# Converting the gated stage's weights beside the experts instead of beside the attention

## The chip, the core and the metric

The kernel runs on one core of one Trainium2 chip, as one launch. The core has a matrix engine (TensorE, PE in the rows), a vector engine (VectorE, DVE), an activation engine (ScalarE, ACT), a general engine (GpSimd, POOL) and a queue engine (SyncE, SP) that issues most DMA transfers. Each of them works through its own queue in program order. The metric is device time in microseconds (us) of the whole launch; every number below is from the kernel before unless it says otherwise.

## What is computed

Three stages follow one another: an attention with pooled queries, a layer of eight experts of which each token takes one, and a gated layer.

```python
# attention: batch 4, heads 8, sequence 1152, head size 64
q_pool = q.reshape(B, H, S // 2, 2, D).mean(axis=3)
scores = np.matmul(q_pool, k.transpose(0, 1, 3, 2)) / np.sqrt(D)
scores = scores - np.max(scores, axis=-1, keepdims=True)
attn = np.exp(scores)
attn = attn / (np.sum(attn, axis=-1, keepdims=True) + 1e-09)
x = np.matmul(attn, v)                  # -> 2304 tokens of 512
# experts: w_gate 512 x 8, w1[e] 512 x 1024, w2[e] 1024 x 512
expert_idx = np.argmax(x @ w_gate, axis=1)
for e in range(8):
    mask = expert_idx == e
    out[mask] = gate_w[mask, None] * (np.maximum(x[mask] @ w1[e], 0.0) @ w2[e])
# gated layer: w_a, w_b 512 x 1536, w_out 1536 x 512
y = ((out @ w_a) * (out @ w_b)) @ w_out
```

The weights w_a, w_b and w_out of the gated layer arrive as float64. [...]

## The kernel before

**Attention.** The 32 heads are handled in 16 pairs of heads (NPAIR), each pair in 21 units (NU), so that 336 units run one after the other. For unit n, TensorE computes scores (`scores`, L335 and L338, PSUM tile sp, two buffers), ScalarE takes the exponential twice, as float32 (L345, tile pt) and as its float16 high half (L347, tile ph), GpSimd subtracts the two to get the low half (`p_low`, L365, tile pl), and four units later TensorE multiplies both halves with the values (`av`, L387). The row maxima of the next pair are found beside that (`a_units`): TensorE computes rough scores (L289) into the PSUM tile sa, which has two buffers, and VectorE reduces each of them to maxima (L294, tile mx). Around this, VectorE also splits keys, values and queries into high and low halves (L228, L214, L242), normalises the results of the pair before (`norm`, `norm_tail`, L407 to L424), and every fourth pair computes the gate (`gate`).

**Conversion.** The three weights are cut into 36 parts of 128 x 512 numbers (`parts`: 12 blocks f, each with m = 0, 1, 2 for w_a, w_b, w_out). For each part SyncE loads the 64-bit words into the tile cl (`conv_load`, L640), ScalarE takes the absolute value of the upper words (`conv_abs`, L649, tile mag), and VectorE runs five instructions: it limits mag (L656), takes the sign from the upper words (L657, tile sgn), adds bits of the lower words (L662), shifts mag (L669) and puts the two together (L674). SyncE then writes the float32 part to a DRAM tile wf (L675). `conv` is a generator with four steps; the call `aside()` in the loop over the units takes one step of the gate, and where no gate is open, one step of the conversion. The list ASIDE holds 0, 1 or 2 for each of the 21 units, 12 steps in all for a pair, from unit 10 on.

**Experts.** The tokens are sorted by expert into slots of 128 (`do_slot`; 18 always run, up to 25 where needed). A slot gathers its tokens (L958, GpSimd's queue), turns them (`x_t`, L971), multiplies by w1 (`stage1`), takes the relu (L991, tile hs), turns the result (`h_t`, L997), multiplies by w2 (`stage2`), scales and scatters (`finish`, L1013, L1014). Each product runs on high and low halves, three matmuls (L977 to L979). The halves come from a cast on ScalarE (hh, xh: L964) and a subtraction on VectorE (hl, xl: L965). Where the next slot has another expert (`changes`), the 16 pieces of its weights are split in the same way (`split_w`: L716 on ScalarE, L720 on VectorE, a quarter of the latter on GpSimd), and the weights after next are loaded (`load_raw`, L141, 1 MB each on SyncE). The first 12 parts of the gated weights (RES = 4 blocks) are read back from wf in slots 0 to 11 (L622, tile pre) and split at the end of the slot (`part_split`, L631 on ScalarE, L632 on VectorE, tile wch, wcl).

**Gated layer.** It runs six blocks of 384 tokens over the 12 blocks f (`ab`, `outs`). The other 24 parts are read back from wf and split while the first block of tokens runs.

The code is issued in the order in which it is written (a manual schedule); no planner reorders it.

## Time and profile before

| what | us |
|---|---|
| median of three runs | 1427.13 (1422.78 to 1430.41) |
| the profiled execution | 1423.17, span 1421.1 |
| attention, from the start to its last pair (from 594.8) | 594.8 |
| last pair, routing, up to the experts' first transposition | 594.8 to 647.7 |
| experts | 647.7 to 948.2 |
| gated layer | 948.2 to 1421.1 |

The profile is one execution with a record for each instruction. TensorE is busy for 90% of the span, VectorE for 59%, ScalarE for 46%, GpSimd for 39%. By 40 equal slices VectorE is at nine tenths through most of the attention and at one to three tenths in the last third. Busy shares of TensorE are to be read with care: its matmuls are pipelined, and their ends are modelled.

### The profile page before, as it was taken

What the parts mean: (1) busy time and instruction counts of PE and PEld (TensorE: products, weight loads), DVE (VectorE), ACT (ScalarE), POOL (GpSimd) and SP (SyncE); (2) the same over time, 40 slices, a digit from 0 to 9 for tenths busy, and PEclk for the clock granted to TensorE, in tenths of its full rate; (3) what the DMA queues carried; (4) which work ended last, traced back from release to release, by engine and by line L of the source; (5) the groups of instructions that cost most, each with busy time, mean ns of one, the idle gap of its engine ahead of it and who ended that gap; (6) DMA issues with size and microseconds to landing.
All of it is one profiled execution on the core that took longest, in us unless ns stands there. A gap on an engine that the chain in (4) does not pass through costs nothing. (4 is left out here: it accounts for less than half of the span.)

```text
span 1421.1 us, 28742 instructions
## 1 busy us (share of the span) xinstructions
PE 1275.9 (90%) x10800; PEld 1018.5 (72%) x10800; DVE 834.0 (59%) x1388; ACT 656.8 (46%) x1295; POOL 556.6 (39%) x467
## 2 busy tenths in 40 slices
PE   8688888878878988858998999989999999999998
PEld 6455555555555555536876887779999999999998
DVE  5689999999998989886279226325322222222211
ACT  3467776766767766834267226224212112111211
POOL 4567787777777777873145113210000000000000
PEclk9999999998999999978999999999999999999999
DMA  6768786567566765134359314424010101010000
GB/s 158 156 158 198 189 223 157 153 161 180 129 153 146 194 141 117 46 136 154 115 178 346 133 47 158 165 70 150 21 45 1 45 1 45 1 45 1 23 0 23
DMA packets 184497, 162.16 MB, mean 114 GB/s; under 512 B 102864, under 2 KB 138192, under 8 KB 184336
## 3 DMA queue, kind: packets, MB, share of 16 engines
q1 hardware_dynamic: 180496, 147.14, 38.1%
q0 software_dynamic: 3840, 13.00, 2.7%
q8 instruction: 86, 1.41, 0.4%
q14 instruction: 75, 0.61, 0.1%
HBM read 106.07 MB, written 25.48 MB: 93 GB/s over the span
## 5 line engine op out<-in xcount | busy, mean ns | idle before, releaser
L365 POOL TENSOR_TENSOR pl<-pt,ph 128x512 f16<-128x512 f32 (+1 forms) x333 | 414.3, 1260 | 167.0 <-ACT ph L347 128.0
L345 ACT ACTIVATE pt<-sp 128x512 f32<-128x512 f32 (+1 forms) x336 | 197.8, 589 | 161.5 <-PE sp L338 150.2
L289 PE MATMUL sa<-kst,qq 128*128 128x384 f16 x480 | 164.2, 342 | 82.8 <-DVE mx L294 78.8
L1144 PE MATMUL ab<-x,wch 128*128 128x384 f32 x1152 | 236.5, 336 | 0.7 <-ACT x L1127 0.7
L294 DVE TENSOR_REDUCE mx<-sa 128x2 f32<-128x768 f32 x224 | 205.4, 922 | 37.3 <-PE sa L289 34.8
L387 PEld LDWEIGHTS <-ph 128*128 128x128 f16 (+1 forms) x2880 | 157.8, 103 | 77.9 <-issue 38.7
L1144 PEld LDWEIGHTS ab<-x,wch 128*128 128x128 f32 x1152 | 202.6, 188 | 5.9 <-ACT x L1127 1.1
L1154 DVE TENSOR_TENSOR gf<-ab,sa 128x384 f32<-128x384 f32 x72 | 40.1, 557 | 272.3 <-PE ab L1144 272.3
L347 ACT ACTIVATE ph<-sp 128x512 f16<-128x512 f32 (+1 forms) x315 | 186.0, 590 | 0.0
L387 PE MATMUL av<-vv,ph 128*128 128x65 f16 (+2 forms) x2880 | 174.9, 199 | 0.0
L289 PE MATMUL sa<-kst,qlt 128*128 128x384 f16 x480 | 164.5, 343 | 0.0
L387 PE MATMUL av<-vv,pl 128*128 128x65 f16 (+1 forms) x1440 | 161.7, 197 | 2.4 <-DVE pl L365 1.7
L335 PE MATMUL sp<-qq,kst 128*128 128x512 f16 (+1 forms) x576 | 141.1, 299 | 10.8 <-ACT ph L347 10.3
L338 PE MATMUL sp<-rl,k2b 66*128 66x512 f16 (+1 forms) x576 | 141.2, 299 | 6.4 <-DMA rl<-qln 6.4
L387 PEld LDWEIGHTS <-pl 128*128 128x128 f16 (+1 forms) x1440 | 126.9, 104 | 2.8 <-DVE pl L365 1.8
L289 PEld LDWEIGHTS <-qlt 128*128 128x128 f16 x480 | 48.3, 101 | 109.4 <-issue 90.4
L1144 PE MATMUL ab<-x,wcl 128*128 128x384 f32 x576 | 123.6, 335 | 0.0
L1153 ACT COPY sa<-ab 128x384 f32<-128x384 f32 x72 | 34.6, 481 | 163.8 <-PE ab L1144 163.8
L1155 ACT CAST gh<-gf 128x384 fp32r<-128x384 f32 x72 | 37.0, 513 | 149.3 <-DVE gf L1154 149.3
L1144 PEld LDWEIGHTS ab<-x,wcl 128*128 128x128 f32 x576 | 103.2, 188 | 0.0
L965 DVE TENSOR_TENSOR hl<-ht,hh 128x512 fp32r<-128x512 f32 x46 | 31.6, 688 | 107.6 <-ACT hh L964 107.6
L1014 POOL DMA_INDIRECT ybuf<-ys,idx x23 | 25.5, 1111 | 165.1 <-DVE ys L1013 122.3
(187 smaller groups left out, 2412.7 us busy)
## 6 DMA issues: line engine op xcount, KB each, us to landing
raw<-in_moe_w_dram SPq DMA_DIRECT2D x36, 1024.0 KB, 6.8
kr<-in_k_dram SPq DMA_DIRECT2D x16, 576.0 KB, 5.2
vr<-in_v_dram SPq DMA_DIRECT2D x16, 576.0 KB, 5.8
wf<-mag SPq DMA_DIRECT2D x36, 256.0 KB, 3.0
qr<-in_q_dram SPq DMA_DIRECT2D x32, 256.0 KB, 3.5
cl<-in_moe_w_a_dram SPq DMA_DIRECT2D x12, 512.0 KB, 4.7
cl<-in_moe_w_b_dram SPq DMA_DIRECT2D x12, 512.0 KB, 3.9
cl<-in_moe_w_out_dram SPq DMA_DIRECT2D x12, 512.0 KB, 3.8
```

The costliest lines, as they stand in the source:

```text
L289: nc.tensor.matmul(sa[:, i, :KA], lhsT=x[:, 128 * b_ : 128 * b_ + 128], rhs=kst[:, j, ks], start=o == 0, stop=o == len(ops) - 1,)
L294: nc.vector.tensor_reduce(out=s["mx"].rearrange("p t n -> p (t n)")[:, ones[0] : ones[0] + m].rearrange("p (m o) -> p m o", o=1), in_=sa[: ...
L335: nc.tensor.matmul(sp[:, o : o + w], lhsT=s["kst"][:, j, ks], rhs=s["qq"][:, c0 : c0 + w], start=True, stop=False)
L338: nc.tensor.matmul(sp[:, o : o + w], lhsT=k2b[p % 3][:, j, ks], rhs=s["rl", j if w > 64 else 1][0:66, c0 : c0 + w], start=False, stop=True,)
L345: nc.scalar.activation(pt[:, :o], sp[:, :o], AF.Exp, scale=1.0 / (16.0 * SC * SC))
L347: nc.scalar.activation(phb[n % NPB][0][:, :o], sp[:, :o], AF.Exp, scale=1.0 / (16.0 * SC * SC))
L365: eng.tensor_tensor(out=l[:, :w], in0=pts.pop(n)[:, :w], in1=h[:, :w], op=ALU.subtract)
L387: nc.tensor.matmul(o, lhsT=a, rhs=b_, start=first, stop=False, skip_group_check=True)
L1144: nc.tensor.matmul(ps[:, 0:TB], lhsT=w_[:, m, 128 * i : 128 * i + 128], rhs=x_[:, i], start=(i + j == 0), stop=(j == 2 and i == KD - 1),)
L1153: nc.scalar.copy(sa, pair[0])
L1154: nc.vector.tensor_tensor(out=gf, in0=pair[1], in1=sa, op=ALU.mult)
L1155: nc.scalar.copy(gh, gf)
```

## The change

The conversion leaves the attention and goes to the experts. `aside` now takes steps of the gate alone. In `do_slot`, a new function `beside(s, 3)` stands at three places (after the first `h_t`, after the second, and behind `finish`) and takes three conversion steps at each for slots 0 to 16, twelve for slot 17. The tiles mag, sgn and cl move to the experts' pools mp and mp2, with two buffers of mag in place of three. Part 0 gets two steps of its own for the first loads and the first Abs. The first 12 parts are no longer written to wf and read back: a fifth step splits them straight from mag with `part_split`. The other 24 still go through wf. The tile pre is gone for this kind of weights.

```diff
--- before.py
+++ after.py
@@ -636,23 +636,31 @@
 
     def conv_load(i):
         f, m = parts[i]
-        t = pst[i] = er2.tile([128, 512], I64, tag="cl", name=f"cl{i}")
+        t = pst[i] = cvp["2"].tile([128, 512], I64, tag="cl", name=f"cl{i}")
         nc.sync.dma_start(out=t.rearrange("p (k f) -> p k f", k=KD) if m < 2 else t, in_=chunk_src(f, m))
 
 
     mags = {}
+    cvp = {}
 
     def conv_abs(i):
         if i < len(parts):
-            mags[i] = er.tile([128, 512], F32, tag=f"mag{i % 3}", name=f"mag{i}")
+            mags[i] = cvp["1"].tile([128, 512], F32, tag=f"mag{i % 2}", name=f"mag{i}")
             bits = pst[i].bitcast(U32).rearrange("p (n w) -> p n w", w=2)
             nc.scalar.activation(mags[i], bits[:, :, 1].bitcast(F32), AF.Abs)
 
+
     def conv(i):
         f, m = parts[i]
+        if i == 0:
+            conv_load(0)
+            conv_load(1)
+            yield
+            conv_abs(0)
+            yield
         bits = pst.pop(i).bitcast(U32).rearrange("p (n w) -> p n w", w=2)
         mag = mags.pop(i)
-        sgn = er.tile([128, 512], U32, tag="sgn", name=f"sgn{i}")
+        sgn = cvp["1"].tile([128, 512], U32, tag="sgn", name=f"sgn{i}")
         nc.vector.tensor_scalar(out=mag, in0=mag, scalar1=W_LO, scalar2=W_HI, op0=ALU.max, op1=ALU.min)
         nc.vector.tensor_scalar(
             out=sgn, in0=bits[:, :, 1], scalar1=0x80000000, scalar2=0x40000000,
@@ -672,19 +680,23 @@
         )
         yield
         nc.vector.tensor_tensor(out=mag.bitcast(U32), in0=mag.bitcast(U32), in1=sgn, op=ALU.bitwise_xor)
-        nc.sync.dma_start(out=wf[f, m], in_=mag)
+        if i < 3 * RES:
+            yield
+            part_split(i, wres, mag)
+        else:
+            nc.sync.dma_start(out=wf[f, m], in_=mag)
         yield
 
 
     gates = []
+
     convs = [conv(i) for i in range(len(parts))] if wide else []
 
-    def aside():
-        for todo in (gates, convs):
-            while todo:
-                if next(todo[0], todo) is None:
-                    return
-                todo.pop(0)
+    def aside(todo=gates):
+        while todo:
+            if next(todo[0], todo) is None:
+                return
+            todo.pop(0)
 
     a_first = [3 * t + n for t in (0, 1, 2, 3) for n in range(3)]
     a_rest = [3 * t + n for t in (4, 5, 6, 7, 8) for n in range(3)]
@@ -818,11 +830,6 @@
                     finish_max(pa, (0, 1) if pa else [1])
             if a_due(n + 1) < a_due(n) + 2 and n + 1 < NPAIR * NU:
                 scores(n + 1)
-            if n == 6 and wide:
-                for i in range(2):
-                    conv_load(i)
-            if n == 9 and wide:
-                conv_abs(0)
             if u == (U["lv"] if p else 5) and nxt:
                 load_v(p + 1)
             for j in range(2):
@@ -894,7 +901,7 @@
                 aside()
             if p == NPAIR - 1:
                 if u == 0:
-                    while gates or convs:
+                    while gates:
                         aside()
                     w1h, w1l, w2h, w2l = open_mw()
                 for i in range(L_H[u], L_H[u + 1]):
@@ -938,6 +945,8 @@
     mp2 = mo_ctx.enter_context(tc.tile_pool(name="mp2", bufs=2))
     mp3 = mo_ctx.enter_context(tc.tile_pool(name="mp3", bufs=4))
     mps = mo_ctx.enter_context(tc.tile_pool(name="mps", bufs=1, space=PSUM))
+    cvp["1"] = mp
+    cvp["2"] = mp2
 
     def split_w(i, ks=(0, 1, 2, 3)):
         for k_ in ks:
@@ -1042,10 +1051,15 @@
                 load_raw(i, next_e(0))
         x_t(0)
         pre = {}
+
+        def beside(s, n):
+            for _ in range(n if s < NT // 128 - 1 else 4 * n if s < NT // 128 else 0):
+                aside(convs)
+
         def do_slot(s):
             if s + 2 < NS:
                 gather(s + 2)
-            if s < 3 * RES:
+            if s < 3 * RES and not wide:
                 pre[s] = mp2.tile([128, 512], F32, tag="pre", name=f"pre{s}")
                 part_src(pre[s], s)
             if s:
@@ -1058,6 +1072,7 @@
                     split_w(3, [0])
             stage1(s, 1, [0, 1])
             h_t(s, 0)
+            beside(s, 3)
             stage1(s, 1, [2, 3])
             if s:
                 with tc.If(changes(s) > 0):
@@ -1065,6 +1080,7 @@
                     load_raw(3, next_e(s))
             stage2(s, [0, 1])
             h_t(s, 1)
+            beside(s, 3)
             if s + 1 < NS:
                 x_t(s + 1)
                 with tc.If(changes(s + 1) > 0):
@@ -1073,8 +1089,9 @@
                         load_raw(i, next_e(s + 1))
             stage2(s, [2, 3, 4, 5, 6, 7])
             finish(s)
-            if s < 3 * RES:
+            if s < 3 * RES and not wide:
                 part_split(s, wres, pre.pop(s))
+            beside(s, 3)
 
         def live(s):
             return nc.values_load(info[0:1, 2, s : s + 1], engines=wengs + [ET.PE], min_val=0, max_val=1)
```

In the rows that follow, names are tiles, with numbers that tell copies apart.

VectorE's queue in the attention, during pair 6, before: mx are the maxima of pair 7, vv and kn the split values and keys, mag, sgn and cl the conversion.

```order
L294 TENSOR_REDUCE mx_4168<-sa_4_4274 128x2
L662 SCALAR_TENSOR_TENSOR sgn_4258<-cl_3878,sgn_4258 128x512
L669 TENSOR_SCALAR mag_4152<-mag_4152 128x512
L674 TENSOR_TENSOR mag_4152<-mag_4152,sgn_4258 128x512
L294 TENSOR_REDUCE mx_4168<-sa_6_4328 128x2
L228 SCALAR_TENSOR_TENSOR kn_4311<-kr_4009,kn_4311 128x9x64
L294 TENSOR_REDUCE mx_4168<-sa_8_4362 128x2
L656 TENSOR_SCALAR mag_4289<-mag_4289 128x512
L657 TENSOR_SCALAR sgn_4376<-cl_4150 128x512
L228 SCALAR_TENSOR_TENSOR kn_4311<-kr_4009,kn_4311 128x9x64
L294 TENSOR_REDUCE mx_4168<-sa_10_4424 128x2
```

The same place after:

```order
L294 TENSOR_REDUCE mx_4010<-sa_4_4111 128x2
L294 TENSOR_REDUCE mx_4010<-sa_6_4157 128x2
L228 SCALAR_TENSOR_TENSOR kn_4142<-kr_3860,kn_4142 128x9x64
L294 TENSOR_REDUCE mx_4010<-sa_8_4191 128x2
L228 SCALAR_TENSOR_TENSOR kn_4142<-kr_3860,kn_4142 128x9x64
L294 TENSOR_REDUCE mx_4010<-sa_10_4250 128x2
```

Five conversion instructions between the reductions are gone; the rest stands in the same order.

VectorE's queue in slot 7 of the experts, from the first half's low part (hl) to the next slot's tokens (xl), before. The rows with a load, a compare and branches are the test whether the expert changes:

```order
L965 TENSOR_TENSOR hl_0_12624<-ht_0_12618,hh_0_12623 128x512
L1029 TENSOR_LOAD info
L1063 COMPARE_AND_BRANCH
L720 TENSOR_TENSOR w2l<-raw_133,w2h 128x512 x2
L1063 UNCONDITIONAL_BRANCH x2
L965 TENSOR_TENSOR hl_1_12679<-ht_1_12673,hh_1_12678 128x512
L965 TENSOR_TENSOR xl_12688<-xt_12682,xh_12687 128x512
```

The same slot after, from the middle of the first three conversion steps to xl:

```order
L682 TENSOR_TENSOR mag_12183<-mag_12183,sgn_12271 128x512
L1038 TENSOR_LOAD info
L1078 COMPARE_AND_BRANCH
L732 TENSOR_TENSOR w2l<-raw_133,w2h 128x512 x2
L1078 UNCONDITIONAL_BRANCH x2
L974 TENSOR_TENSOR hl_1_12416<-ht_1_12410,hh_1_12415 128x512
L664 TENSOR_SCALAR mag_12359<-mag_12359 128x512
L665 TENSOR_SCALAR sgn_12419<-cl_12181 128x512
L670 SCALAR_TENSOR_TENSOR sgn_12419<-cl_12181,sgn_12419 128x512
L677 TENSOR_SCALAR mag_12359<-mag_12359 128x512
L974 TENSOR_TENSOR xl_12434<-xt_12428,xh_12433 128x512
```

Conversion instructions now stand in front of the weight split (w2l), of hl and of xl.

ScalarE's queue in slot 6, from the first half's cast (hh) to the next slot's tokens (xh), before:

```order
L964 CAST hh_0_12398<-ht_0_12393 128x512
L991 ACTIVATE hs_1_12408<-hp_1_12386 128x512
L1029 TENSOR_LOAD info
L1063 COMPARE_AND_BRANCH
L716 CAST w2h<-raw_133 128x512 x3
L1063 UNCONDITIONAL_BRANCH x2
L964 CAST hh_1_12453<-ht_1_12448 128x512
L964 CAST xh_12462<-xt_12457 128x512
```

The same slot after; wch is the high half of a part, cast from mag:

```order
L973 CAST hh_0_12110<-ht_0_12105 128x512
L650 ACTIVATE mag_12116<-cl_11936 128x512
L631 CAST wch_12024<-mag_11938 128x512
L1000 ACTIVATE hs_1_12128<-hp_1_12098 128x512
L1038 TENSOR_LOAD info
L1078 COMPARE_AND_BRANCH
L728 CAST w2h<-raw_133 128x512 x3
L1078 UNCONDITIONAL_BRANCH x2
L973 CAST hh_1_12173<-ht_1_12168 128x512
L650 ACTIVATE mag_12183<-cl_12114 128x512
L973 CAST xh_12191<-xt_12186 128x512
```

An Abs and the cast of a part now stand in front of the relu (hs), and a second Abs in front of xh.

## Rows read from the trace of the kernel before

**Rows 1.** The page: span, and busy time of each engine.
```profile
span 1421.1 us, 28742 instructions
PE 1275.9 (90%) x10800; PEld 1018.5 (72%) x10800; DVE 834.0 (59%) x1388; ACT 656.8 (46%) x1295; POOL 556.6 (39%) x467
```
**Rows 2.** Busy time by stretch: pairs 1 to 14, experts.
```profile
core 0: us, PE busy (x) PEld busy (x) DVE busy (x) ACT busy (x) POOL busy (x), PEclk, DMA share, GB/s
78.40:594.80 516.40, 429.96 (x5920) 282.98 (x5917) 478.83 (x800) 366.13 (x746) 387.19 (x311) 0.93 0.64 159
647.70:948.20 300.50, 289.65 (x1385) 234.24 (x1384) 147.95 (x189) 132.51 (x240) 90.52 (x73) 1.00 0.45 154
```
**Rows 3.** Waits, 78.4 to 594.8: who for whom, total us, times, longest.
```profile
PE sa L289 <- DVE mx L294: 73.2, 55, 3.9
```
**Rows 4.** Timeline in pair 6, VectorE then TensorE: start, us, instruction, idle before.
```profile
270.90 0.94 DVE L294 TENSOR_REDUCE mx<-sa 128x2 f32<-128x768 f32 x1
271.76 0.51 DVE L656 TENSOR_SCALAR mag<-mag 128x512 f32<-128x512 f32 x1
272.20 1.63 DVE L657 TENSOR_SCALAR sgn<-cl 128x512 uint32<-128x512 uint32 x1
273.74 1.72 DVE L228 SCALAR_TENSOR_TENSOR kn<-kr,kn 128x576 f16<-128x576 f32 x1
275.38 0.94 DVE L294 TENSOR_REDUCE mx<-sa 128x2 f32<-128x768 f32 x1
...
276.38 0.48 PE L289 MATMUL sa<-kst,qq 128*128 128x384 f16 x1 [2.06 <-DVE mx L294]
```
**Rows 5.** Busy time by stretch, columns as in rows 2: pairs 6, 9, 14.
```profile
262.40:301.00 38.60, 30.46 (x428) 20.09 (x424) 37.70 (x57) 26.62 (x55) 28.52 (x23) 0.96 0.65 157
378.70:414.90 36.20, 30.08 (x429) 19.92 (x425) 32.47 (x62) 25.95 (x54) 26.94 (x23) 0.95 0.62 134
562.80:594.80 32.00, 28.00 (x416) 18.62 (x413) 27.96 (x47) 23.50 (x47) 25.26 (x21) 0.95 0.28 80
```
**Rows 6.** Busy time of the instructions on mag (first) and on cl alone.
```profile
core 0: us, DVE busy (x) ACT busy (x), PEclk, DMA share, GB/s
78.40:594.80 516.40, 90.43 (x104) 23.15 (x34) 0.93 0.64 159
...
78.40:594.80 516.40, 71.72 (x70) 23.15 (x34) 0.93 0.64 159
```
**Rows 7.** The five conversion instructions by line: shortest/median/longest ns, first and last start.
```profile
L656 DVE TENSOR_SCALAR mag<-mag x36: 416/522/1380, 60.5 to 577.2; 128x512 f32<-128x512 f32 x36
L657 DVE TENSOR_SCALAR sgn<-cl x36: 412/1370/1634, 60.9 to 577.6; 128x512 uint32<-128x512 uint32 x36
L662 DVE SCALAR_TENSOR_TENSOR sgn<-cl,sgn x36: 674/696/1667, 66.2 to 581.4; 128x512 uint32<-128x512 uint32 x36
L669 DVE TENSOR_SCALAR mag<-mag x36: 410/697/1399, 74.1 to 583.8; 128x512 uint32<-128x512 uint32 x36
L674 DVE TENSOR_TENSOR mag<-mag,sgn x36: 676/762/1659, 74.5 to 590.8; 128x512 uint32<-128x512 uint32 x36
```
**Rows 8.** Experts: two slots' transpositions (timeline), then stretches with columns as in rows 2.
```profile
816.38 0.60 PE L971 MATMUL xt<-ident,xg 128*128 128x128 f32 x4
828.71 0.60 PE L971 MATMUL xt<-ident,xg 128*128 128x128 f32 x4
...
684.50:721.50 37.00, 37.00 (x183) 30.72 (x182) 9.99 (x15) 10.45 (x18) 6.45 (x6) 1.00 0.20 60
721.48:779.06 57.58, 51.80 (x242) 39.99 (x241) 55.92 (x67) 47.49 (x88) 32.81 (x24) 1.00 0.85 298
657.49:684.50 27.01, 25.25 (x122) 20.26 (x121) 18.48 (x22) 15.09 (x28) 10.62 (x8) 1.00 0.65 226
865.69:893.26 27.57, 25.67 (x123) 20.14 (x122) 25.08 (x31) 22.38 (x42) 15.21 (x12) 1.00 0.73 247
```
**Rows 9.** Cast and split of a part (ns); weights' landing (KB, us); cl landing (us).
```profile
L631 ACT CAST wch<-pre x12: 616/620/624, 662.9 to 805.4; 128x512 fp32r<-128x512 f32 x12
L632 DVE TENSOR_TENSOR wcl<-pre,wch x12: 676/680/683, 666.0 to 809.5; 128x512 fp32r<-128x512 f32 x12
raw<-in_moe_w_dram SPq DMA_DIRECT2D x36, 1024.0 KB, 6.8
DMA to landing us min/median/max: 3.4/4.0/8.3
```

## What the change was predicted to do

> **What bounds the kernel now.** I read the page first: what the span is made of [rows 1]. Then the busy times of the stretches [rows 2]. Attention pairs 1 to 14 (78.4 to 594.8 us, from pair 1's first exponential to pair 15's) take 516.4 us, 36.9 a pair. VectorE is busy for 478.83 of it (93%), TensorE for 429.96, GpSimd for 387.19, ScalarE for 366.13. In the experts (647.7 to 948.2) TensorE is busy for 289.65 of 300.50 us and VectorE for half of it. So the two stages have different limits, and the change carries work from one to the other.
>
> A busy share alone proves no limit, so the waits come next [rows 3]: TensorE stands idle for 86.4 us of those pairs, and 73.2 us of it are waits of the maxima's matmul (L289) for VectorE's reduction (L294), which must free one of its two PSUM buffers. One such place in order of time [rows 4]: the reduction that starts at 270.90 is followed by L656, by L657 (1.63 us) and by a weight split (1.72 us); the next reduction starts at 275.38, and TensorE, which had stood for 2.06 us, goes on at 276.38. The two conversion instructions delayed it by about 2 us. That is the pattern to see: a queue in program order, with work in front of the reduction that nobody waits for.
>
> A natural comparison supports it [rows 5]. Pair 6, with a full load of conversions: 38.60 us, VectorE 37.70 busy. Pair 9, where gate steps take the place of some conversions: 36.20 with 32.47. Pair 14, with nothing left to prepare for later pairs: 32.00 with 27.96. The time follows VectorE's load at a slope of about 0.7 (6.6 us for 9.7).
>
> **What leaves the attention.** 36 parts, five VectorE instructions and one Abs each, 36 loads and 36 stores. VectorE's share is 90.43 us on the tile mag and 71.72 on cl (no instruction is in both) [rows 6]: 162 us in pairs 1 to 14, 11.6 a pair. Left to VectorE are (478.8 - 162.2) / 14 = 22.6 us a pair. It can no longer be the limit. What is late next: TensorE with 429.96 / 14 = 30.7 busy, GpSimd with 27.7, ScalarE with 26.2 less 1.7 for the Abs. I take 30.7: all of TensorE's idle time goes, its clock stays. That saves 86 us. The bounds: pair 14's 32.0, with VectorE still at 87%, would give 69; half of the maxima's waits left (they come in bursts, where splits and normalisations stand together) would cut the saving to some 50. Above: the clock of this stretch is 0.93 [rows 2]; at 1.00 the 430 us of TensorE become 400, and the saving 116. The middle of 50 and 116 is near 86. Six of the 180 conversion instructions lie outside these pairs, at 0.93 us each (162.15 / 174): up to 5 us, I take 2. SyncE's queue loses 72 issues there, which I count at nothing, since all of TensorE's idle time is in the sum already.
>
> **What the experts get: the price.** In the attention one part costs 4.66 us of VectorE. Its fastest copies cost 0.416 + 0.412 + 0.674 + 0.410 + 0.676 = 2.59 us [rows 7], while single copies of the same instruction run to 1.4 or 1.6 us. GpSimd is busy for 75% of the pairs, but for 30% of the experts, so I price the part there at 2.59, 0.65 a step. The Trainium skill (SBUF — State Buffer, section "SBUF: two separate sides") says that VectorE in a two-port mode, or with two SBUF inputs, and GpSimd exclude each other for a whole instruction; the trace agrees as far as the two levels of L657 (0.412 and 1.37) show it. By this rule 36 parts cost 93 us in the experts, without it 168.
>
> **The price on the path.** The steps are 12 x 5 + 24 x 4 + 2 = 158; at 9 a slot they fill slots 0 to 16, and 5 go to slot 17. Nine steps are 5.8 us; the split of the first 12 parts was in the slots before (0.68 us [rows 9]), so the slots up to 11 gain 5.2. A slot that keeps its expert takes 12.33 us [rows 8], and VectorE is busy for 9.99 in three of them: 3.3 + 5.2 fits below 12.33, at no cost, with TensorE's matmuls (37.00 us busy of 37.00) as the cover. Where the expert changes, 22 weight splits come in. In the chain of four changes (721.48 to 779.06) VectorE is busy for 55.92 of 57.58 us, so that nothing covers the addition: 4 x 5.2 - 1.7 = 19 us. The first change (657.49 to 684.50) has lost 2.4 us against two plain slots already, with VectorE at 18.48; between 0 and 10, I take 3. The two late changes (865.69 to 893.26, VectorE 25.08 of 27.57) get 8 steps, 5.2 us, less 2.5 of room: 3.
>
> ScalarE is the second queue. The cast of a part (0.62 us) used to read a tile that a DMA had brought; it now waits for VectorE's last step of that part, with the relu, the transposed halves and the next expert's casts queued behind it, and TensorE behind those. 12 times between 0 and 1.3 us (cast and split); I take 0.6, 7 us. Each Abs waits for a load issued only one part ahead, 4 steps or 5.5 us in a plain slot; the landing takes 3.4 to 8.3 us, median 4.0, and the weights' transfers in front of it 6.8 [rows 9]. About 14 of the 36 lie near a change: 0 to 2.8 us each, I take 0.6, 8 us. The stores go from 36 to 24, the reads in this stage from 12 to none ahead of slot 15; nobody waits for them.
> Together 19 + 3 + 3 + 7 + 8 = 40 us. Bounds: 15 (the late and first changes free, half of the chain hidden, no ScalarE stall) and 75 (the chain at 1.17 a step as in the attention, +20, and the ScalarE stalls doubled).
>
> **Sum.** The profiled execution took 1423.17 us (span 1421.1): 1423.2 - 86 - 2 + 40 = 1375. The median of the three runs is 1427.13, 4.0 above it, so the forecast is 1379. The last stage keeps its instructions and its length.
>
> **Rivals.**
> A: TensorE's clock comes back as well. In the pairs it falls from 2.4 to 1.2 GHz after the waits (granted share 0.93); in the experts, where it idles for 10.9 us in all, it is 1.00 [rows 2]. Without the waits a pair takes 28.6: 30 us less, 1349. Against it: GpSimd's 27.7 and ScalarE's 24.5 stand so close to 28.6 that some wait of theirs will appear. The Trainium skill (TensorE: Matmul & The Clock Gate, section "HAM oscillation — how this bites in real kernels") says that idle gaps put the array back to the half clock; by that rule this case gets likelier, and the change chain of the experts, with longer gaps, dearer.
> B: GpSimd takes over in the pairs. Each exponential's low half (L365) is GpSimd's, and TensorE's last products need it. If the pair stops at 33.3, the saving is 50: 1415. For it: 27.7 busy of 30.7 leaves little slack. Against: without the conversions its own instructions get shorter.
> C, slower: every Abs of the experts waits for its load, since the queue of SyncE issues it behind the weights' loads, and all of ScalarE stands behind it. At 8.3 - 5.5 = 2.8 us for each of 36 that is 101 us in place of 8: 1472. From a mean wait of 1.6 us on ((48 + 8) / 36) the change loses. Against it: plain slots have no load of weights in the queue.
> D, also slower: the change doesn't do what it says, since the maxima's waits stay for another reason and the pairs save 10 us instead of 86: about 1455. [rows 3, 4] speak against it.
>
> **How the numbers follow.** Forecast 0.64 (1355 to 1405 by its own bounds), A 0.15, B 0.12, C 0.06, D 0.03. The range leaves out C and D and a little of each end: 1340 to 1412. About 0.5% can be told from no change, so faster means under 1420: the forecast, A and half of B give 0.85; the better rest of B 0.05 for the same; C, D and the tail of B 0.10 for slower.
>
> **What would show it.** Right: pairs of 29 to 33 us, TensorE's wait for the reduction under 20 us in total, VectorE at 70 to 75% there; plain slots still at 12.33 or within 0.5; the change chain some 20 us longer with VectorE full. Wrong: pairs over 34 us with GpSimd or ScalarE named as the releaser of TensorE (B), Abs instructions of the experts with idle time put down to cl (C), plain slots over 13 us (the cover is gone), or a granted clock under 0.9 in the change slots.

## The result: 1387.5 us, and where the time went

The changed kernel takes 1387.49 us (median of four runs, 1386.30 to 1388.60), the kernel before 1425.35 beside it (1422.78 to 1430.41). The ratio is 0.973, with a 95% interval of 0.970 to 0.976. The forecast was 1379, its range 1340 to 1412.

The profiled execution after took 1388.60 us. Its span is 1386.5 us, where it was 1421.1 [rows 1]; VectorE is busy for 778.5 us of it, where it was 834.0.

The busy times by stretch of after, with the columns of [rows 2]: pairs 1 to 14; the experts from their first to their 24th transposition; in them the chain of four changes, the first change, and the late changes (they answer to [rows 8]):

```profile
74.90:510.10 435.20, 401.48 (x5921) 267.64 (x5918) 336.97 (x624) 346.91 (x713) 358.00 (x310) 0.99 0.58 126
562.80:909.50 346.70, 304.86 (x1365) 237.78 (x1364) 235.36 (x366) 151.87 (x274) 89.26 (x73) 0.96 0.59 197
644.70:730.30 85.60, 63.42 (x242) 45.61 (x241) 77.18 (x109) 50.77 (x95) 31.97 (x24) 0.88 0.78 265
572.40:606.90 34.50, 28.40 (x122) 21.56 (x121) 27.50 (x41) 17.83 (x33) 9.91 (x8) 0.90 0.61 200
824.20:859.20 35.00, 28.10 (x123) 21.35 (x122) 33.39 (x45) 23.75 (x44) 15.25 (x12) 0.95 0.75 263
```

And the experts of before between the same two events:

```profile
647.70:943.40 295.70, 284.92 (x1364) 230.61 (x1364) 146.63 (x186) 131.43 (x238) 90.52 (x73) 1.00 0.46 156
```

Set against rows 2 and 8, these lines split the 34.6 us of span. Pairs 1 to 14 fall from 516.4 to 435.2 us (-81.2, now 31.1 a pair). What lies before pair 1 falls from 78.4 to 74.9 (-3.5). The experts rise from 295.7 to 346.7 (+51.0). The passage from the attention to the experts (-0.2) and all behind the 24th transposition (-0.7) stay. Of the experts' 51 us the chain has 28.0 (85.6 for 57.6), the first change 7.5 (34.5 for 27.0), the late changes 7.4 (35.0 for 27.6); 8 are left for all other slots, 3 of them in the slot behind the chain and 5 spread over plain slots, of which some still take 12.33 us and the longest 13.55.

In the attention, the waits of after for [rows 3] and its neighbours (who for whom, total us, times, longest):

```profile
ACT pt L345 <- PE sp L338: 79.1, 115, 3.9
DVE mx L294 <- PE sa L289: 72.7, 85, 2.7
PE sa L289 <- DVE mx L294: 21.2, 21, 2.5
```

The direction has turned: the reduction now waits 72.7 us for TensorE, where it had waited 24.2 (ScalarE waited for TensorE before as well, 133.8 us, and now 79.1). TensorE is idle for 435.2 - 401.5 = 33.7 us, where it was 86.4. Its busy time fell as well, by 28.5 us with the same matmuls, since the granted clock rose from 0.93 to 0.99. So 52.7 us of the gain are waits and 28.5 are clock. Pair by pair the rest is uneven; here pair 9, in which gate steps run, and pair 10, in which none do (they answer to [rows 5]):

```profile
323.60:359.80 36.20, 30.05 (x427) 19.70 (x424) 28.87 (x57) 24.96 (x52) 25.77 (x23) 0.95 0.55 111
359.80:389.10 29.30, 28.32 (x429) 18.94 (x426) 22.22 (x40) 24.96 (x52) 24.79 (x22) 1.00 0.60 120
```

Pair 9 took 36.20 us before as well [rows 5], with VectorE at 32.47 in place of 28.87. So it gained nothing, and the comparison of pairs 6, 9 and 14, from which I read a slope of 0.7, doesn't hold for a pair with gate steps.

In the experts of after, the waits of ScalarE and those for it:

```profile
ACT mag L650 <- DMA wf<-mag: 43.6, 17, 5.4
ACT wch L631 <- DVE mag L682: 23.9, 8, 6.2
PE yp L988 <- DVE hl L974: 15.0, 6, 4.6
PE ht L1006 <- ACT hs L1000: 9.2, 5, 4.3
ACT mag L650 <- DMA cl<-in_moe_w_a_dram: 6.8, 2, 4.0
```

The first line is the surprise. The Abs of part i + 1 writes the buffer of mag that part i - 1 used, since there are two, and must wait until the store of part i - 1 to wf has left it: 43.6 us of waits on ScalarE. For loads of cl the largest entry is 6.8.

How a cast of a part holds TensorE up is to be seen in one slot of the chain. Timeline of after, in order of time (start, us, instruction, idle before):

```profile
670.22 5.91 DVE L732 TENSOR_TENSOR w1l<-raw,w1h 128x512 fp32r<-128x512 f32 x6
...
676.72 0.68 DVE L682 TENSOR_TENSOR mag<-mag,sgn 128x512 uint32<-128x512 uint32 x1
...
677.43 0.62 ACT L631 CAST wch<-mag 128x512 fp32r<-128x512 f32 x1 [3.73 <-DVE mag L682]
677.95 2.17 ACT L728 CAST w2h<-raw 128x512 fp32r<-128x512 f32 x4
...
680.03 0.59 ACT L1000 ACTIVATE hs<-hp 128x512 f32<-128x512 f32 x1
...
680.67 1.11 PE L1006 MATMUL ht<-ident,hs 128*128 128x128 f32 x4 [4.35 <-ACT hs L1000]
```

VectorE reaches the last step of a part (676.72) only behind six weight splits. ScalarE stands for 3.73 us in front of the cast that needs it; the next expert's casts and the relu (hs) are queued behind; TensorE stands for 4.35 us until the relu is done. Before, this cast read a tile that a DMA had brought, and all twelve together stood 2.0 us for it. Whether the cast's wait makes the chain longer is another question; late_cast, further down, takes it away.

### The profile page after: what moved, and what is told of

It is laid out like the page before. It is cut to its first block, busy times and chain, and to the rows that moved or that the text cites. A ratio compares the mean times of both kernels' runs of the same rounds, so it can differ in the third digit from the quotient of the medians.

```text
span 1386.5 us, 28562 instructions
## 1 busy us (share of the span) xinstructions
PE 1268.5 (91%) x10800; PEld 1010.5 (73%) x10800; DVE 778.5 (56%) x1388; ACT 657.1 (47%) x1295; POOL 524.7 (38%) x467
## 5 line engine op out<-in xcount | busy, mean ns | idle before, releaser
L365 POOL TENSOR_TENSOR pl<-pt,ph 128x512 f16<-128x512 f32 (+1 forms) x333 | 388.1, 1182 | 113.0 <-ACT ph L347 80.3
L387 PEld LDWEIGHTS <-ph 128*128 128x128 f16 (+1 forms) x2880 | 151.3, 101 | 75.8 <-issue 33.8
L289 PE MATMUL sa<-kst,qq 128*128 128x384 f16 x480 | 159.1, 332 | 27.8 <-DVE mx L294 24.5
L387 PE MATMUL av<-vv,ph 128*128 128x65 f16 (+2 forms) x2880 | 168.7, 196 | 0.0
L387 PE MATMUL av<-vv,pl 128*128 128x65 f16 (+1 forms) x1440 | 156.1, 194 | 4.2 <-POOL pl L365 2.5
L289 PE MATMUL sa<-kst,qlt 128*128 128x384 f16 x480 | 159.0, 332 | 0.0
L338 PE MATMUL sp<-rl,k2b 66*128 66x512 f16 (+1 forms) x576 | 137.0, 292 | 8.8 <-DMA rl<-qln 8.3
L335 PE MATMUL sp<-qq,kst 128*128 128x512 f16 (+1 forms) x576 | 136.6, 291 | 7.0 <-ACT ph L347 7.0
L1170 ACT COPY sa<-ab 128x384 f32<-128x384 f32 x72 | 34.6, 481 | 163.8 <-PE ab L1161 163.8
L988 PE MATMUL yp<-w2h,hl 128*128 128x512 f32 x184 | 75.7, 412 | 15.0 <-DVE hl L974 15.0
L1188 PE MATMUL o<-wch,gl 128*128 128x512 f32 x216 | 85.5, 396 | 0.0
```

Source lines behind the costliest of these rows:

```text
L289: nc.tensor.matmul(sa[:, i, :KA], lhsT=x[:, 128 * b_ : 128 * b_ + 128], rhs=kst[:, j, ks], start=o == 0, stop=o == len(ops) - 1,)
L335: nc.tensor.matmul(sp[:, o : o + w], lhsT=s["kst"][:, j, ks], rhs=s["qq"][:, c0 : c0 + w], start=True, stop=False)
L338: nc.tensor.matmul(sp[:, o : o + w], lhsT=k2b[p % 3][:, j, ks], rhs=s["rl", j if w > 64 else 1][0:66, c0 : c0 + w], start=False, stop=True,)
L365: eng.tensor_tensor(out=l[:, :w], in0=pts.pop(n)[:, :w], in1=h[:, :w], op=ALU.subtract)
L387: nc.tensor.matmul(o, lhsT=a, rhs=b_, start=first, stop=False, skip_group_check=True)
L988: nc.tensor.matmul(ps, lhsT=al, rhs=bh_, start=False, stop=last)
```

## The experiments

Each kernel ran beside the kernel before (median 1424 to 1427 us in these groups of runs). The parts with the same code vary a little from kernel to kernel: pairs 1 to 14, the same in all variants of after but the two with added load, took 435 to 441 us. Differences of a few us in the total are therefore read from the stage that was edited.

**What the conversion costs in all** (no_conv, from the kernel before):

```diff
-            nc.sync.dma_start(out=t, in_=wf[f, m])
+            nc.sync.dma_start(out=t, in_=w2[f % 8][128 * m : 128 * m + 128])
-    convs = [conv(i) for i in range(len(parts))] if wide else []
+    convs = []
...
```

> The kernel before with the conversion left out: no loads of the 64-bit words, no Abs, no VectorE steps, no stores; the parts that the gated layer needs are read from an expert's float32 weights instead, so the output is not the reference's. Theory (VectorE's load held the attention, and the conversion is what the experts now pay for): pairs 1 to 14 take 31 us each as after the change (435 us), the experts 300 us as before it, the whole about 1427 - 84 = 1340 us, 50 us under the changed kernel. Rival (something else in the experts got slower, such as the pools' new places): the experts stay near 345 us only where that something is in the kernel, so 300 here says nothing against it, but pairs over 33 us would say that the attention gained from more than the conversion's leaving.

Measured: 1341.86 us (1340.99 to 1344.33), ratio 0.941 (0.936 to 0.945). Its pairs 1 to 14 and its experts:

```profile
75.00:511.60 436.60, 403.79 (x5919) 269.02 (x5916) 336.86 (x624) 347.05 (x713) 358.18 (x311) 0.98 0.57 126
564.40:861.50 297.10, 285.99 (x1363) 231.52 (x1363) 145.45 (x186) 131.50 (x238) 89.53 (x73) 0.99 0.46 156
```

The pairs are those of after to 1.4 us, the experts those of before to 1.4 us. So the conversion cost 83 us beside the attention (79.8 in the pairs and 3.4 before them), all of that is gone after, and it costs 50 us beside the experts (346.7 for 297.1; 46 between the medians of the whole). What still keeps a pair at 31.1 us has nothing to do with it.

**Queue or port: VectorE's load put back** (load_reduce, load_port, both from after). At the 12 places of a pair where conversion steps used to stand, one instruction on tiles of its own: a reduction with a single SBUF input in the one kernel, a multiply-add from SBUF to SBUF in the other.

```diff
...
+                if p < NPAIR - 1:
+                    nc.vector.tensor_reduce(out=dz1, in_=dz[:, 0:512], axis=AX.X, op=ALU.max)
```

```diff
...
+                if p < NPAIR - 1:
+                    nc.vector.tensor_scalar(out=dz2, in0=dz, scalar1=1.0, scalar2=2.0, op0=ALU.mult, op1=ALU.add)
```

> The changed kernel with 12 extra VectorE instructions in each attention pair but the last (a maximum over 512 float32 of a tile in SBUF that nothing else uses, written to one column, about 0.65 us each), where the conversion's steps used to be: one input, one element a cycle, so nothing that GpSimd would have to share. Theory (VectorE's queue time is what held the pairs): 7.8 us of load on 24.1 brings VectorE back to its limit, pairs 33 to 34.5 us against 31.1, +28 to +48 in all. Rival (the conversions cost the attention by shutting GpSimd out): no load on GpSimd, pairs within 0.7 us of 31.1.

> The same with 12 multiply-adds by constants over 1024 float32, SBUF to SBUF, nominally as long (about 0.68 us, by the 0.41 us that 512 take at best), of the kind of L656 and L657. Theory (VectorE's load): they take about 1.2 to 1.6 us each beside GpSimd, as L656 and L657 did, so pairs of 35 to 38 us, as long as before the change. Rival (only the nominal work counts): the same pairs as with the reductions. GpSimd's own low halves (L365) rise from 1.18 us towards 1.28 on average.

Measured: load_reduce 1441.19 us (ratio 1.010), load_port 1502.47 (1.053). Pairs 1 to 14 of load_reduce; the added instruction and GpSimd's subtraction there (busy us, mean ns | idle before); TensorE's wait for the reduction; then the first three lines again, of load_port, where this wait is 90.6 us:

```profile
76.30:562.10 485.80, 423.62 (x5918) 277.95 (x5915) 432.91 (x795) 348.61 (x712) 358.17 (x310) 0.94 0.50 114
L908 DVE TENSOR_REDUCE dz<-dz 128x1 f32<-128x512 f32 x172 | 116.5, 678 | 1.5
L370 POOL TENSOR_TENSOR pl<-pt,ph 128x512 f16<-128x512 f32 x253 | 299.0, 1194 | 123.0 <-ACT ph L352 88.1 <-PE sp L343 17.0 <-PE av L392 7.2
PE sa L294 <- DVE mx L299: 43.5, 36, 4.0
```

```profile
75.70:620.00 544.30, 438.85 (x5922) 287.40 (x5919) 498.49 (x795) 349.62 (x713) 405.78 (x310) 0.92 0.45 101
L908 DVE TENSOR_SCALAR dz<-dz 128x1024 f32<-128x1024 f32 x169 | 173.4, 1026 | 1.5
L370 POOL TENSOR_TENSOR pl<-pt,ph 128x512 f16<-128x512 f32 x252 | 333.2, 1335 | 133.1 <-ACT ph L352 97.0 <-issue 11.8 <-PE sp L343 10.4
```

Work that nobody waits for, put back in front of the reductions, brings the wait (43.5 us, where after had 21.2), the loss and the lower clock back (0.94, 0.92). A pair takes 34.7 and 38.9 us, in both a little over what I had expected. The pairs grow by 50.6 us for 95.9 us more of VectorE's busy time, and by 109.1 for 161.5: slopes of 0.53 and 0.68. The removal of the conversion had 81.2 for 141.9, which is 0.57. So the load in VectorE's queue is the cause: the reductions alone bring the loss back, though they leave GpSimd's own work as it was. The second kernel adds a cause of its own: the reduction leaves GpSimd's subtraction at 1194 ns (1202 in after), but the multiply-add lengthens it to 1335 ns. The Trainium skill (SBUF — State Buffer, section "Who interferes with whom") says that a reduction never takes the port pair that VectorE shares with GpSimd, while a multiply-add of this kind can; these two lines agree.

**A third buffer of mag** (mag3, from after; the gathered tokens get three buffers in place of four to make room):

```diff
-            mags[i] = cvp["1"].tile([128, 512], F32, tag=f"mag{i % 2}", name=f"mag{i}")
+            mags[i] = cvp["1"].tile([128, 512], F32, tag=f"mag{i % 3}", name=f"mag{i}")
```

> The changed kernel with three buffers of mag in place of two, paid for with one buffer less of the gathered tokens (three in place of four). Theory (the Abs that wait for a store of their own tile, 14.0 us in the chain of changing slots, hold ScalarE and with it TensorE): these waits go, 6 to 14 us shorter. Rival (VectorE is full there anyway, and ScalarE's stalls only fill its idle time): 0 to 3 us.

Measured: 1388.38 us (1386.95 to 1389.56), no gain in the whole, as the rival had it; the experts, which were edited, take 342.3 us for 346.7. The Abs' waits for loads in its experts:

```profile
ACT mag L650 <- DMA cl<-in_moe_w_b_dram: 12.5, 5, 6.6
ACT mag L650 <- DMA cl<-in_moe_w_out_dram: 11.5, 7, 3.5
ACT mag L650 <- DMA cl<-in_moe_w_a_dram: 7.6, 4, 3.3
```

The wait for the store is gone, and the Abs waits for its load instead, 31.6 us. One wait had hidden the other. The cast's wait stays (24.7 us).

**The steps moved out of the change slots** (plain_only, from after; plain_mag3 is the same with the third buffer). The slots are those without a change of expert for the inputs of this case, so the numbers hold for its routing alone.

```diff
-            for _ in range(n if s < NT // 128 - 1 else 4 * n if s < NT // 128 else 0):
+            for _ in range(5 if s in (2, 3, 4, 10, 11, 12, 13, 14, 15) else 12 if s == 16 else 0):
```

> The changed kernel with the same conversion steps taken only in slots that neither change nor prepare a change of the expert with these inputs (15 a slot in slots 2, 3, 4 and 10 to 15, the rest in 16), none in slots 0, 1, 5 to 9. Theory (the cost sits where VectorE has no room): the chain of four changes returns from 86 to 58 us and the first change from 34 to 27; the plain slots now hold 15 x 0.65 = 9.8 us and 3.3 of their own, 13.1, and take 13 to 15 us each (+8 to +25 in all); the experts end near 315 to 325 us, the whole 20 to 30 us under the changed kernel. Rival (the conversion costs the same wherever in the experts it stands, since it loads the queues of ScalarE and SyncE): within 5 us of the changed kernel.

> The kernel that converts in plain slots only, with three buffers of mag (and three of the gathered tokens). There the plain slots took 16 to 20 us, with 47.5 us of ScalarE's waits put down to the store of a tile that the next Abs writes to. Theory (that store, and then the load one part ahead, limits a part to 4.5 us, three or four parts a slot): with the store out of the way plain slots take 13 to 16 us, the whole 15 to 30 us less than 1405. Rival (15 steps of VectorE a slot are too many whatever the buffers): 1400 or more.

Measured: plain_only 1405.31 us (ratio 0.985), 18 us longer than after, where my theory had it shorter; plain_mag3 1396.44 (0.978). The four changes did go back to 13 to 14.5 us a slot (but for the fourth of plain_only with 17.5, which took 16.6 in no_conv too), but the full plain slots took 16.3 to 20.1 (15.4 to 18.7 in plain_mag3), and slot 16 with the 23 steps that were left over 24.2 (23.4). A stretch of plain slots of plain_only with slot 16 at its end, and the Abs' waits for stores in all its experts (in plain_mag3 they wait for loads instead, 20.9 + 16.1 + 14.2 = 51.2 us):

```profile
735.00:840.00 105.00, 77.61 (x326) 58.64 (x325) 69.31 (x135) 30.71 (x51) 12.46 (x11) 0.90 0.61 196
ACT mag L650 <- DMA wf<-mag: 52.8, 17, 4.8
```

VectorE is busy for 69 of 105 us: the steps would fit. It is ScalarE's queue that stands: busy for 31 us, it waits 47.5 us of this stretch in front of one Abs after the other, and the matmuls' operands stand behind it (TensorE waits 20.2 us for that queue). The theory that VectorE's time alone bounds a plain slot fell; with the steps closer together, each Abs meets its store or its load.

**ScalarE taken out of the way** (abs_dve3: after with three buffers and the absolute value as a bit operation on VectorE; late_cast: abs_dve3 with the cast and the low half of a part three and four steps behind the step that they need).

```diff
-            nc.scalar.activation(mags[i], bits[:, :, 1].bitcast(F32), AF.Abs)
+            nc.vector.tensor_scalar(
+                out=mags[i].bitcast(U32), in0=bits[:, :, 1], scalar1=0x7FFFFFFF, scalar2=None, op0=ALU.bitwise_and
+            )
```

```diff
-        if i < 3 * RES:
-            yield
-            part_split(i, wres, mag)
+        if direct(i - 1):          # three steps behind, in the next part
+            part_high(i - 1, pool or wres, mags[i - 1])
...
+        if direct(i - 1):          # one step later
+            part_low(i - 1, mags.pop(i - 1))
```

> The changed kernel with the Abs moved from ScalarE to VectorE (a bitwise and, 0.41 us, as the first instruction of its part instead of one part ahead), three buffers of mag, three of the gathered tokens. Theory (in the experts ScalarE's stalls on loads and stores of the conversion cost some 20 of the 51 us): VectorE's load in a slot rises from 5.8 to 6.8 us, yet the experts get shorter, 320 to 338 us in place of 347; plain slots 12.33, the chain of four 78 to 84 in place of 86. Rival (VectorE's time sets the chain): 4 us longer there, the whole 0 to 6 us longer.

> The kernel with the Abs on VectorE and three buffers of mag, and the cast of each of the first 12 parts put three steps after the part's last VectorE step, its low half four steps after, so that ScalarE finds the tile ready. Theory (ScalarE's waits for VectorE's last step, 35.0 us in the experts of that kernel, hold relu and weight casts): they fall under 10 us, the experts get 5 to 15 us shorter, the whole 1368 to 1378 against 1382.5. Rival (VectorE's own added time is all that is left): within 3 us of 1382.5.

Measured: abs_dve3 1382.54 us (1382.13 to 1383.00), ratio 0.969 (0.966 to 0.973); late_cast 1378.78 (1376.57 to 1384.19), 0.968, between its theory and its rival. Their experts take 336.9 and 333.0 us, against 346.7 in after, though VectorE now does the absolute values too. The cast's wait in abs_dve3, its chain of changes and its late changes; then the same three lines of late_cast (its lines are numbered anew):

```profile
ACT wch L631 <- DVE mag L683: 35.0, 8, 7.3
648.30:730.80 82.50, 61.52 (x242) 45.78 (x241) 79.05 (x117) 47.30 (x87) 31.34 (x24) 0.85 0.82 275
818.68:853.77 35.09, 28.10 (x123) 21.30 (x121) 34.44 (x48) 23.08 (x42) 14.38 (x11) 0.90 0.71 244
```

```profile
ACT wch L638 <- DVE mag L697: 3.9, 3, 1.8
652.07:737.21 85.14, 61.65 (x243) 48.22 (x242) 82.66 (x121) 46.73 (x85) 31.80 (x24) 0.85 0.83 281
824.45:851.96 27.51, 25.51 (x122) 20.15 (x121) 24.23 (x30) 21.75 (x41) 14.90 (x11) 1.00 0.73 256
```

The Abs' waits on ScalarE were worth at least the 9.8 us that the experts of abs_dve3 lost: 3.1 of them in the chain, and four plain slots of 13.1 to 13.6 us are back at 12.33. The cast's wait is another matter. Late_cast takes it away, and the chain gets no shorter (85.1 us for 82.5), nor does the first change (34.7 for 32.9). The gain of late_cast over abs_dve3 lies in the late changes, 27.5 us for 35.1. There it has another reason: the cast and the low half no longer have steps of their own, so 145 steps are to be taken in place of 158, and the last conversion instruction ends at 823.4 us, before these changes begin; abs_dve3 and after still convert in them. So no run shows that the cast's wait costs time by itself; late_cast also gives VectorE 3.6 us more to do in the chain. What is left in the chain is VectorE, busy for 97% of it.

**Plain slots again, with ScalarE free** (plain_late, plain_late4, from late_cast; again for the routing of these inputs):

```diff
+            for _ in range(5 if s in (2, 3, 4, 10, 11, 12, 13, 14, 15) else 12 if s == 16 else 0):
```

```diff
+            for _ in range(4 if s in (2, 3, 4, 10, 11, 12, 13, 14, 15, 16) else n if s in (5, 9) else 12 if s == 17 else 0):
```

> Late_cast (1378.8 us) with the steps moved within the experts: fifteen steps in each slot that has no change of expert for the inputs of this case (slots 2, 3, 4 and 10 to 15), the rest in slot 16. This is plain_only again, but with the Abs on VectorE and the casts late, so that ScalarE waits for nothing of the conversion. Theory (plain_only failed since ScalarE's queue waited for stores and loads, not for lack of VectorE time): a plain slot needs VectorE for 3.3 + 15 x 0.75 = 14.6 us, so slots of 14 to 15 us instead of 12.3 (nine of them, +18 to +24), against the four-slot chain back from 85 to about 58 us and the first change from 34 to 28: a kernel of 1360 to 1372 us. Rival (so many steps at once are bound by the loads and stores of their data, as in plain_only and plain_mag3): plain slots of 16 us and more, a kernel of 1385 us or longer.

> As plain_late, but twelve steps in each of the slots 2 to 4 and 10 to 16, nine in slots 5 and 9 and the rest in slot 17. Theory (only VectorE's time bounds these slots): 3.3 + 12 x 0.75 = 12.3 us fits a plain slot, so plain slots of 12.3 to 13 us and the chain near 58 us: a kernel of 1352 to 1366 us, shorter than plain_late by 5 us or more. Rival (bound by loads and stores): plain slots of 14 us and more, a kernel of 1375 us or longer, within 5 us of plain_late or over it.

Measured: plain_late 1385.17 us (ratio 0.972), the number of the rival; plain_late4 1372.28 (1370.54 to 1373.52), ratio 0.964 (0.960 to 0.967), between both. A plain slot of plain_late, then one of plain_late4 and its worst slot:

```profile
604.13:621.91 17.78, 14.42 (x63) 11.20 (x62) 15.16 (x31) 5.14 (x9) 2.60 (x2) 0.90 0.50 150
```

```profile
723.33:736.50 13.17, 12.62 (x62) 10.10 (x61) 10.83 (x23) 2.87 (x5) 2.33 (x2) 1.00 0.67 223
803.60:827.01 23.41, 16.04 (x63) 12.15 (x62) 23.02 (x36) 11.49 (x21) 8.79 (x6) 0.84 0.77 260
```

The rival's reason is not the one: the conversion instructions of plain_late wait for loads or stores for 1.1 us in all. In its first plain slot VectorE's steps run in a row (start, us, instruction; the rows between them, left out, are conversion steps as well):

```profile
606.11 0.42 DVE L660 TENSOR_SCALAR mag<-cl 128x512 uint32<-128x512 uint32 x1
...
610.76 0.69 DVE L992 TENSOR_TENSOR xl<-xt,xh 128x512 fp32r<-128x512 f32 x1
...
611.56 0.50 PE L1005 MATMUL hp<-w1l,xh 128*128 128x512 f32 x1 [2.46 <-DVEq L1104]
```

From 606.11 to 610.76 the conversion has VectorE's queue for itself; the next tokens' low half (xl) comes behind it, and TensorE stands for 2.46 us. ScalarE was not as free as I had meant it to be: in the first three full slots the cast still waits for VectorE's last step, 15.5 us in plain_late and 18.8 in plain_late4. In the later plain slots this wait is gone, and those with 15 steps still take 14.5 to 16.8 us. So the bunch counts, not only the sum: with 15 steps a plain slot takes 14.5 to 17.8 us, with 12 it takes 13.2 to 14.4, against 12.33 with none. Plain_late4 is the shortest kernel here that does the whole work, 15 us below after. It has two slots of 20.4 and 23.4 us, where steps of slot 5, and those of slot 16 with the last seven, stand beside the next expert's weight splits; what a better placing gives wasn't tried.

**A part of the work moved on** (gated12, from late_cast: the last 12 parts are converted in the first block of the gated layer, and six steps a slot are left in the experts; the preparation of the next block's tokens, `x2_part`, moves there from blocks 5, 7 and 9 to 8, 9 and 10).

```diff
-            for _ in range(n if s < NT // 128 - 1 else 4 * n if s < NT // 128 else 0):
+            for _ in range(n - 1 if s < NT // 128 - 1 else 4 * n if s < NT // 128 else 0):
...
+            if n == 0:
+                for _ in range(6 if f < 3 else 9):
+                    aside(late)
```

> late_cast with the last 12 of the 36 parts converted during the first block of the gated layer (six to nine steps beside each of its first steps, VectorE busy for a fifth there), split straight from mag; the experts take six steps a slot in place of nine. Theory (what is left in the experts is VectorE's time in changing slots): chain of four 6 to 10 us shorter than in late_cast, the first and the late changes 1 to 3 each, the gated layer at 462 us as before (its cover is TensorE's matmuls, 9.2 us a step): 8 to 16 us less than late_cast. Rival (the gated layer's first block has no room either, since each of its steps waits for splits in VectorE's queue): the gated layer longer by as much, 465 to 475.

Measured: 1394.19 us (ratio 0.979). The experts fall to 322.5 us (-10.5 against late_cast), the gated layer rises to 490.5 from 464.5, more than the rival had it. In its first block:

```profile
ACT gh L1203 <- DVE gf L1202: 37.3, 11, 9.4
PE o L1217 <- ACT gh L1203: 18.2, 6, 6.6
ACT wch L638 <- DVE mgb L697: 16.3, 8, 3.0
```

TensorE waits for ScalarE's cast gh. Gh waits for VectorE's product gf, which is queued behind conversion steps, and that is the larger wait; the casts of the parts, queued in front of the next gh, wait for VectorE too.

**The direct split alone** (wf_all_b, from after: all 36 parts go through wf, the first 12 read back in slots 3 to 14).

```diff
-        if i < 3 * RES:
-            yield
-            part_split(i, wres, mag)
-        else:
-            nc.sync.dma_start(out=wf[f, m], in_=mag)
+        nc.sync.dma_start(out=wf[f, m], in_=mag)
```

> The changed kernel with one part of it undone: no part is split straight from mag; all 36 go to DRAM, and the first 12 are read back into a tile of one buffer and split in slots 3 to 14 (three buffers of the gathered tokens to make room). Theory (a cast that waits for VectorE's last step holds ScalarE): those waits (23.9 us in the experts of the changed kernel) go, but the Abs of the first 12 parts now wait for stores as the other 24 do (43.6 us there): between 10 us shorter and 6 us longer than 1387.5. Rival (VectorE's time sets the experts): the same number of its instructions, within 3 us.

Measured: 1391.71 us (1389.83 to 1393.43), 4 above after; its experts take 345.5 us for 346.7, and its pairs happen to take 438.2 for 435.2. The whole hides two effects here: without the fifth steps of twelve parts the conversion ends before the late changes, and they take 27.4 us for 35.0, but the chain takes 89.9 for 85.6 and the other slots 2 more. So this run doesn't price the splitting at once by itself; it shows that the gain doesn't need it. The move to the experts is the change.

## Why the prediction was right, and where its steps were off

**What bounds the attention: right.** The reductions waited behind VectorE's conversion; no_conv and the two load kernels show it from both sides. Pairs with gate steps are an exception: pair 9 kept its 36.2 us. Rival D is out.

**The attention's term: 86 and 2 forecast, 81.2 and 3.5 measured, but for other reasons.** I let all of TensorE's idle time go and kept its clock. In fact 33.7 of 86.4 us of idle time stayed, and the clock rose to 0.99. TensorE's 401.48 us, 28.7 a pair, are what rival A said to a tenth; its 1349 us failed since the waits did not all go. Two errors cancelled: 52.7 of 86.4 for the waits, 28.5 for a clock that I had counted at nothing. That their sum came so close to 86 is luck. What stays of waits is mostly still the reduction's (21.2 us, just over the 20 named as the sign), most of all in pairs with gate steps. The Trainium skill (TensorE: Matmul & The Clock Gate, section "HAM oscillation — how this bites in real kernels") lets the clock fall after idle gaps; here it rose where the gaps went and fell where they came, to 0.88 in the chain of changes that had 1.00. I cited the rule and gave it too little weight on both sides.

**VectorE's remaining load: 22.6 us a pair forecast, 24.1 measured.** I subtracted the conversion's busy time from the total. But busy times don't add: in [rows 4] each instruction starts 0.07 to 0.09 us before the one in front of it has ended. With 176 instructions go 176 such overlaps, by estimate 12 to 16 of the 20.3 us between the 162.2 that I subtracted and the 141.9 that went; the rest was not traced. So VectorE is busy for 77% of the pairs, where I had named 70 to 75.

**The price of a part beside the experts: right.** Forecast 2.59 us, from the fastest copies. The five lines in the experts of after (count | busy, mean ns | idle before):

```profile
L664 DVE TENSOR_SCALAR mag<-mag 128x512 f32<-128x512 f32 x36 | 15.3, 424 | 1.9 <-ACT mag L650 1.9
L665 DVE TENSOR_SCALAR sgn<-cl 128x512 uint32<-128x512 uint32 x36 | 16.2, 449 | 0.0
L670 DVE SCALAR_TENSOR_TENSOR sgn<-cl,sgn 128x512 uint32<-128x512 uint32 x36 | 24.8, 689 | 0.8
L677 DVE TENSOR_SCALAR mag<-mag 128x512 uint32<-128x512 uint32 x36 | 15.2, 422 | 0.0
L682 DVE TENSOR_TENSOR mag<-mag,sgn 128x512 uint32<-128x512 uint32 x36 | 24.8, 688 | 0.8
```

They sum to 2.67 us a part. The price was 4.66 in the attention, beside a GpSimd that is busy for 75% of the time, and is this beside one that is busy for 26%; the same work is 72 us cheaper on VectorE.

**The price on the path: 40 forecast, 51 measured.** The term that was mis-sized is the chain, 19 forecast and 28.0 measured. VectorE's part of it was right: 77.18 for 55.92 us busy, +21.3 where 4 x 5.2 = 20.8 was counted. Wrong was that the 1.7 us of room would be used up: VectorE's idle time there rose to 8.4 us, since it waits for ScalarE while ScalarE waits for it; with the Abs off ScalarE it is 3.5 (abs_dve3). On TensorE's side the 28 us are 16.4 more of idle time and 11.6 of half clock. The first and the late changes were put at 3 us each and took 7.5 and 7.4; the bounds of the first (0 to 10) held it. In the first, VectorE is busy for 27.50 of 34.50 us, and ScalarE stands 8.5 us for VectorE's last steps and 4.0 for a load. In the late ones VectorE is full (33.39 of 35.00) and has 8.3 us more to do, where 5.2 was counted. The plain slots were put at nothing and cost 5, so "12.33 or within 0.5" held for most and not for all; with the Abs off ScalarE 4 of these 5 us are gone (abs_dve3).

**ScalarE: the Abs by another wait, the casts not shown.** I gave 7 us to the casts and 8 to the Abs, by the landing of loads. The Abs stood for 43.6 us on stores, which I had dismissed with "nobody waits for them": two buffers of mag make the Abs of part i + 1 wait for the store of part i - 1. Taking the Abs off ScalarE was worth 9.8 us of the experts, with VectorE carrying it on top. The casts stood for 23.9 us, but with their wait taken away neither the chain nor the first change got shorter, so their 7 us are not shown. Rival C, every Abs behind its load, showed its mechanism only where the store's wait was taken away (mag3: 31.6 us), and then without further loss.

**Rival B** did not come: GpSimd's low half is no releaser of TensorE's worth naming, and its instruction stayed near 1.2 us.

**The signs.** Two of the signs that I named for being wrong came in part: the clock fell to 0.88 in the chain, and four plain slots took over 13 us. They point at costs that the sum held too low, and not at a change that loses.

**The base.** I added 4 us since the profiled execution of before lay that far below the median; the profiled one of after lies 1 above its median. Of the 8.5 us by which the forecast was too low, the experts have 11 and the attention 3 in the one direction, this and small terms some 6 in the other.

## What to carry to other kernels

Work that nobody waits for is not free in a queue in program order: move it to a stage where its engine and its port partner are quiet, and place it a few instructions at a time; placing it behind what the bounding engine needs next, and not before, follows from the waits seen here but was not tried. When a wait on a loaded tile becomes a wait on another engine, list what is queued behind the waiting instruction; and when a buffer is written by one engine and stored by a DMA, count the store among the waits of the next writer. A wait that is removed may only uncover the next one (store, then load, then cast), so a single repair that brings nothing does not clear the engine. And a variant that needs fewer steps ends earlier: compare stage by stage, before its gain is put down to the wait that it was built to remove.

## What the runs showed of the hardware that I had not expected

The same number of VectorE's instructions costs its neighbours very different amounts. Twelve reductions a pair (678 ns each) left GpSimd's subtraction at 1194 ns and made the pair 3.6 us longer; twelve multiply-adds made it 7.8 us longer, raised the subtraction to 1335 ns and took 1026 ns each themselves, where half the columns take 424 ns in the experts (L664), so that 850 would be an estimate for the whole without GpSimd. And removing the waits gave a third of the attention's gain through the clock alone: 28.5 of 81.2 us with the same matmuls.
